# Float32r passes in place of float32 matmuls for the last four score loads of the first batch

## The chip, the cores and the metric

The kernel runs on one core of a Trainium2 chip. The metric is the device time of one execution in microseconds (us); a profile of one execution shows what each engine did in it.

## What is computed

The reference takes `q`, `k` and `v` of 4 batches with 6080 tokens and 256 channels. It attends over channels, not tokens, and sends the result through a feed-forward layer of width 2048:

```python
qn = q / (np.linalg.norm(q, axis=1, keepdims=True) + 1e-06)
kn = k / (np.linalg.norm(k, axis=1, keepdims=True) + 1e-06)
s = kn.transpose(0, 2, 1) @ qn / tau          # 256 x 256 for each batch
a = softmax of s over its last axis
x = (v @ a).reshape(24320, 256)
h = x @ w_in                                  # 256 x 2048
out = (0.5 * h * (1 + erf(h / sqrt(2)))) @ w_out
```

## The kernel before

Work is done batch by batch. For a batch the scores `k^T q` are summed over the tokens, the softmax gives a 256 x 256 matrix, and that matrix is multiplied into `w_in` (`w_group`), so that the tokens of `v` need two products only: the first with the combined weights, then gelu, then the second with `w_out`. The tokens go in six pairs of up to 512-column tiles, and the 2048 hidden channels in 8 units. Products are made of float32r passes: each operand is held as `hi` (the value rounded to float32r, by a copy) and `lo` (the rest, by a subtraction), and three passes lo x hi, hi x hi, hi x lo stand for one float32 product. A float32r pass is one matmul record in the profile; a whole float32 matmul is two.

The scores of batches 1 to 3 are made in this way beside the products of the batch before (`split_qk`, `burst`, lines 178 to 201). Those of the first batch have nothing to run beside. They are made at the start, in a loop of 24 steps (`js`, lines 607 to 620), one for each load of 512 KB (256 tokens of q and k) into a buffer `raw0`, of which there are 13. Step `js` calls `qk_first` (lines 142 to 153): four whole float32 matmuls of 256 columns (line 149) into two PSUM tiles, and for `js` below 20 (`NSQ`) also `squares` (lines 131 to 139): ScalarE squares the load (line 138) and VectorE adds the squares up (line 139). The norms of the tokens of the last four loads come from elsewhere: four pieces of a transposed copy (`norm_part`, line 208 the load, line 209 ScalarE's square with its sum), in a buffer `kq0` of which there are three. Step `js` then issues load `js + 13` (the last four of these are the first loads of batch 1), and at certain steps a norm piece (2, 4, 6, 8), v (5) or a unit of weights (10, 13, 15). Weights come as 64-bit numbers; `narrow` (lines 221 to 251) turns a unit into `hi` and `lo` by a chain of VectorE and ScalarE operations. Steps 14 to 17 also split the first tile pair of v (`v_split`, ScalarE's cast at line 445, VectorE's subtraction at line 446).

After the loop come three more weight units, and `softmax` in stages (line 278): the squares are summed on TensorE (`sum_up`, line 172, held behind the last score matmul), and a chain of small steps on VectorE, ScalarE and TensorE leads to the matrix `eh`, `el`. Between the stages TensorE does part of the scores of batch 1 (`qk_fill`, line 161). Then `w_group` (lines 376 to 379) and the first products (lines 458 to 460), gelu (lines 466 to 468) and the second products (lines 541 to 543) follow, and go on until the end.

All loads and stores are issued from SyncE's queue, in order. The order of an engine's instructions is fixed when the program is built: a scheduler takes, of those whose operands are ready by its own reckoning, the one that comes first in the program.

Of the kernel before, what the change touches and what calls it, by code (L numbers as in the profile page):

```python
# [10 lines left out]
F32R = mybir.dt.float32r  # L11
U32 = mybir.dt.uint32
AF = mybir.ActivationFunctionType
ALU = mybir.AluOpType
AX = mybir.AxisListType

P = 128
B, N, C = 4, 6080, 256
DFF = 2048
NT = 512  # L20
NJ = -(-N // P)
NFT = DFF // P
NCT = C // P
# [7 lines left out]
JS = 2  # L31
# [11 lines left out]
NSQ = 5 * NSJ  # L43
# [9 lines left out]
B11, B21, B22, T1, T2, T3, T4 = range(7)  # L53

A21, B12 = -1, T1
# [5 lines left out]
def channel_attention_gelu_ffn(ctx, tc, qk, kqt, vt, tau, w_in, w_out, out):  # L61
# [11 lines left out]
    nc = tc.nc  # L73
# [5 lines left out]
    pqk = ctx.enter_context(tc.tile_pool(name="pqk", bufs=2))  # L79
# [10 lines left out]
    pst = pstart.__enter__()  # L90

    def f32(ap):
        return ap.bitcast(F32)
# [6 lines left out]
    state = {}  # L100

    marks = {}
# [8 lines left out]
    def bank():  # L111
        return ps_h.tile([P, NT], F32, name="ph")


    raws = {}

    def load_first(i):

        b, js = divmod(i, NQS)
        raw = pst.tile([P, JS, 2, C], F32, name="raw0", bufs=AHEAD)  # L120
        step = 1 if i == 0 else JS
        for j in range(0, JS, step):
            marks["loads"] = nc.sync.dma_start(out=raw[:, j:j + step], in_=qk[b, :, js * JS + j:js * JS + j + step])
        raws[b, js] = raw
# [6 lines left out]
    def squares(js, raw):  # L131
        if js == 0:
            state["acc"] = pst.tile([P, JS, 2, C], F32, name="acc")
            nc.scalar.activation(out=state["acc"], in_=raw, func=AF.Square)
            return
        acc = state["acc"]
        sq = pst.tile([P, JS, 2, C], F32, name="sq", bufs=2)
        nc.scalar.activation(out=sq, in_=raw, func=AF.Square)
        nc.vector.tensor_tensor(out=acc, in0=acc, in1=sq, op=ALU.add)  # L139


    def qk_first(js):
        if js == 0:
            state["s"] = [bank()[:, 0:C] for m in range(NCT)]
        s = state["s"]
        raw = raws.pop((0, js))
        for j in range(JS):
            for m in range(NCT):
                marks["scores"] = nc.tensor.matmul(  # L149
                    s[m], raw[:, j, 0, m * P:(m + 1) * P], raw[:, j, 1],  # L150
                    start=(js == 0 and j == 0), stop=(js * JS + j == NJ - 1), skip_group_check=True)
        if js < NSQ:
            squares(js, raw)

    def qk_fill():
        state["fill"] = s = ps_o.tile([P, NCT, C], F32, name="po")
# [46 lines left out]
    def norm_part(b, t, c):  # L203

        if "nsum" not in state:
            state["nsum"] = pm.tile([P, 2 * NCT, 8], F32, name="nsum")
        x = pst.tile([P, NS], F32, name="kq0", bufs=3) if b == 0 else pg.tile([P, NS], F32, name="kqc", bufs=2)
        nc.sync.dma_start(out=x, in_=kqt[b, t, :, c * NS:(c + 1) * NS])
        nc.scalar.activation(out=x, in_=x, func=AF.Square, accum_out=state["nsum"][:, t, c:c + 1])  # L209
# [199 lines left out]
    def load_v(b, p):  # L409
        t0, n = PAIRS[p]  # L410
        raw = pv.tile([P, NCT, 2 * NT], F32, name="v_raw")
        nc.sync.dma_start(out=raw[:, :, :2 * n],
                          in_=vt[:, b * N + t0:b * N + t0 + 2 * n].rearrange("(t p) n -> p t n", p=P))
        vraw[b, p] = raw

    def v_blocks(b, p):
        n = PAIRS[p][1]
        raw = vraw[b, p]
        return {(k, j): raw[:, k, j * n:(j + 1) * n] for k in range(2) for j in range(2)}
# [15 lines left out]
    def v_split(b, p, i):  # L435
        n = PAIRS[p][1]
        x = v_blocks(b, p)
        src = {B11: x[0, 0], B21: x[1, 0], B22: x[1, 1]}.get(i)
        if (b, p, i) == (0, 0, B12):
            src = x[0, 1]  # L440
        if src is None:
            src = vts[b, p][i - T1][:, :n]
        hi = pv.tile([P, NT], F32R, name=f"vh{i}")
        lo = pv.tile([P, NT], F32R, name=f"vl{i}")
        nc.scalar.copy(out=hi[:, :n], in_=src)
        nc.vector.tensor_tensor(out=lo[:, :n], in0=src, in1=f32(hi[:, :n]), op=ALU.subtract)
        vops[b, p, i] = hi, lo
# [113 lines left out]
    def load_unit():  # L561
        kind, g, d = units.pop(0)
        src = w_in64[:, d, g * NT:(g + 1) * NT] if kind == "in" else w_out64[:, g * 2 * C:(g + 1) * 2 * C]
        loaded.append((kind, g, d, load_w(src)))
# [11 lines left out]
    def narrow_unit():  # L576
        kind, g, d, raw = loaded.popleft()
        if kind == "in":
            if d == 0:
                new_win(0, g)  # L580
            win = wins[0, g]
            narrow(win[:, 0, d], win[:, 1, d], raw)
            if d == NCT - 1:
                keep(keep_in[g], win)
        else:
            new_wo((0, 0, g))
            wo = wos[0, 0, g]
            narrow(wo[:, 0].rearrange("p f c -> p (f c)"), wo[:, 1].rearrange("p f c -> p (f c)"), raw)
            keep(keep_out[g], wo)
# [17 lines left out]
    for js in range(NQS):  # L607
        qk_first(js)
        if js + AHEAD < NQS + FILL:
            load_first(js + AHEAD)  # L610
            if js in (2, 4, 6, 8):
                norm_part(0, *pieces.pop(0))
            if js == 5:
                load_v(0, 0)
        if js in (10, 13, 15):
            load_unit()
        if js in NARROWS:
            narrow_unit()
        if 14 <= js < 18:
            v_split(0, 0, (B11, B21, B12, B22)[js - 14])  # L620
    for _ in range(3):
        narrow_unit()
    for x in held:
# [136 lines left out]
```

## Time and profile before

| | us |
|---|---|
| median of 3 runs | 2186.55 |
| lowest and highest run | 2185.65, 2186.91 |
| the profiled execution | 2186.79 |
| its span, first to last instruction | 2185.0 |
| TensorE busy in it | 2174.5 |
| VectorE busy | 1392.8 |
| ScalarE busy | 1437.0 |

PE is TensorE's matmuls, PEld its weight loads, DVE VectorE, ACT ScalarE, SPq SyncE's queue of transfers. Matmul records overlap their neighbours, so the pace of a series is read from the starts. Times in rows are us from the start of the span, unless marked otherwise.

### The profile page before, as it was taken

Reading aid. Unit: us, or ns where it says so; the run is one execution under the profiler, and the core shown is the slowest. Engines: PE = TensorE matmul, PEld = TensorE weight load, DVE = VectorE, ACT = ScalarE, POOL = GpSimd, SP = SyncE. Lnnn points to the kernel's source line nnn. Section 1 sums busy time; section 2 is a strip of 40 time slices with the busy share of each in tenths; the row PEclk is TensorE's granted clock in tenths of the full one; section 3 lists DMA queues with packets and bytes.
Section 4 is the critical chain, followed back from the end, with each engine's and each line's share of the span. In section 5 each row is a group of like instructions: output and inputs, shape, how many; then the busy total and the mean of one; then the engine's idle time right before and its main releaser. Section 6 shows DMA issues by size and latency. Waiting matters only on the chain.

```text
span 2185.0 us, 26209 instructions
## 1 busy us (share of the span) xinstructions
PE 2174.5 (100%) x9664; PEld 1793.9 (82%) x9664; DVE 1392.8 (64%) x2179; ACT 1437.0 (66%) x2595; POOL 1.3 (0%) x8
## 2 busy tenths in 40 slices
PE   9999999999999999999999999999999999999999
PEld 7788888888888888888888888888888888888888
DVE  6995767656676575675667757657466555555554
ACT  6666666667666666676765666667576566666665
POOL 0000000000000000000000000000000000000000
PEclk9999999999999999999999999999999999999999
DMA  9562534422343353542323335343132122121121
GB/s 380 189 211 106 174 133 157 160 90 87 106 144 105 118 173 116 174 154 67 105 92 134 122 116 174 133 153 128 49 112 97 58 89 71 65 97 66 68 78 47
DMA packets 77056, 267.52 MB, mean 122 GB/s; under 512 B 7680, under 2 KB 9728, under 8 KB 74880
## 3 DMA queue, kind: packets, MB, share of 16 engines
q1 hardware_dynamic: 76928, 265.84, 35.2%
q8 instruction: 76, 1.25, 0.2%
q14 instruction: 52, 0.43, 0.1%
HBM read 232.52 MB, written 33.29 MB: 122 GB/s over the span
## 4 chain that ended last, share of the span: by engine, by line
PE 97%; DVE 2%; DMA 1%; issue 0%; ACT 0%; SPq 0%; DVEq 0%; ACTq 0%
PE po L543 16%; PE po L541 16%; PE po L542 16%; PE ph L460 14%; PE ph L459 14%; PE ph L458 14%; PE ph L191 3%; PE ph L193 1%; DMA raw<-qk 1%; DVE acc L139 1%; PE ph L378 1%; PE ph L376 1%; PE ph L377 1%; PE ph L149 0%; DVE nt L247 0%
## 5 line engine op out<-in xcount | busy, mean ns | idle before, releaser
L468 DVE TENSOR_TENSOR gl<-g,gh 128x512 fp32r<-128x512 f32 (+1 forms) x768 | 521.7, 682 | 145.3 <-ACT g L467 142.7
L543 PE MATMUL po<-gl,wo 128*128 128x512 f32 (+1 forms) x1536 | 605.2, 394 | 0.0
L541 PE MATMUL po<-gh,wo 128*128 128x512 f32 (+1 forms) x1536 | 599.2, 390 | 0.6 <-ACT gh L466 0.6
L542 PE MATMUL po<-gh,wo 128*128 128x512 f32 (+1 forms) x1536 | 595.6, 388 | 0.0
L496 DVE TENSOR_TENSOR h<-ph,p 128x512 f32<-128x512 f32 (+1 forms) x368 | 252.0, 685 | 531.4 <-PE ph L460 452.6
L460 PE MATMUL ph<-vl,wh 128*128 128x512 f32 (+1 forms) x1336 | 522.7, 391 | 0.0
L459 PE MATMUL ph<-vh,wh 128*128 128x512 f32 (+1 forms) x1336 | 521.5, 390 | 0.0
L458 PE MATMUL ph<-vh,wl 128*128 128x512 f32 (+1 forms) x1336 | 519.8, 389 | 0.7 <-DVE wl L363 0.7
L466 ACT ACTIVATE gh<-h 128x512 fp32r<-128x512 f32 (+1 forms) x552 | 345.2, 625 | 236.8 <-DVE h L496 232.8
L491 ACT COPY p<-ph 128x512 f32<-128x512 f32 (+1 forms) x368 | 213.4, 583 | 241.4 <-PE ph L460 240.3
L542 PEld LDWEIGHTS po<-gh,wo 128*128 128x128 f32 x1536 | 288.4, 188 | 64.0
L541 PEld LDWEIGHTS po<-gh,wo 128*128 128x128 f32 x1536 | 288.4, 188 | 62.3 <-ACT gh L466 1.0
L543 PEld LDWEIGHTS po<-gl,wo 128*128 128x128 f32 x1536 | 288.4, 188 | 61.5
L467 ACT ACTIVATE g<-h 128x512 f32<-128x512 f32 (+1 forms) x552 | 337.5, 611 | 0.0
L459 PEld LDWEIGHTS ph<-vh,wh 128*128 128x128 f32 x1336 | 251.1, 188 | 56.9
L458 PEld LDWEIGHTS ph<-vh,wl 128*128 128x128 f32 x1336 | 251.0, 188 | 53.2 <-DVE h L496 1.4
L460 PEld LDWEIGHTS ph<-vl,wh 128*128 128x128 f32 x1336 | 250.9, 188 | 51.0
L491 ACT COPY u<-ph 128x512 f32<-128x512 f32 (+1 forms) x184 | 106.9, 581 | 106.6 <-PE ph L460 106.6
L466 ACT ACTIVATE gh<-ph 128x512 fp32r<-128x512 f32 (+1 forms) x216 | 125.3, 580 | 22.9 <-PE ph L460 18.2
L467 ACT ACTIVATE g<-ph 128x512 f32<-128x512 f32 (+1 forms) x216 | 126.5, 586 | 1.6 <-DVE gl L468 1.5
L496 DVE TENSOR_TENSOR h<-ph,u 128x512 f32<-128x512 f32 (+1 forms) x184 | 125.4, 682 | 2.8
L209 ACT ACTIVATE kqc<-kqc 128x1024 f32<-128x1024 f32 x72 | 76.4, 1061 | 36.1 <-DMA kqc<-kqt 36.0
(135 smaller groups left out, 1354.0 us busy)
## 6 DMA issues: line engine op xcount, KB each, us to landing
wo<-keep_out SPq DMA_DIRECT2D x184, 512.0 KB, 3.3
raw<-qk SPq DMA_DIRECT2D x95, 512.0 KB, 4.3
kqc<-kqt SPq DMA_DIRECT2D x72, 512.0 KB, 4.4
v_raw<-vt SPq DMA_DIRECT2D x20, 1024.0 KB, 5.5
out<-osb SPq DMA_DIRECT2D x40, 512.0 KB, 3.3
win<-keep_in SPq DMA_DIRECT2D x12, 1024.0 KB, 4.8
keep_in<-win SPq DMA_DIRECT2D x4, 1024.0 KB, 4.6
keep_out<-wo SPq DMA_DIRECT2D x8, 512.0 KB, 3.6
```

What stands on the lines that cost most here:

```text
L209: nc.scalar.activation(out=x, in_=x, func=AF.Square, accum_out=state["nsum"][:, t, c:c + 1])
L458: nc.tensor.matmul(ps[:, :n], wl, hi[:, :n], start=start, stop=False, skip_group_check=True)
L459: nc.tensor.matmul(ps[:, :n], wh, hi[:, :n], start=False, stop=False, skip_group_check=True)
L460: marks["product"] = nc.tensor.matmul(ps[:, :n], wh, lo[:, :n], start=False, stop=stop, skip_group_check=True)
L466: nc.scalar.activation(out=gh[:, :n], in_=src, func=AF.Gelu)
L467: marks["gelu"] = nc.scalar.activation(out=g[:, :n], in_=src, func=AF.Gelu)
L468: nc.vector.tensor_tensor(out=gl[:, :n], in0=g[:, :n], in1=f32(gh[:, :n]), op=ALU.subtract)
L491: nc.scalar.copy(out=t[:, :n], in_=ps[:, :n])
L496: nc.vector.tensor_tensor(out=h[:, :n], in0=ps[:, :n], in1=t[:, :n], op=ALU.add)
L541: nc.tensor.matmul(o, wo[:, 1, i, cs], gh[:, :n], start=first, stop=False)
L542: nc.tensor.matmul(o, wo[:, 0, i, cs], gh[:, :n], start=False, stop=False)
L543: nc.tensor.matmul(o, wo[:, 0, i, cs], gl[:, :n], start=False, stop=last)
```

## The change

The last four loads of the first batch (`js` 20 to 23) are split into `hi` (ScalarE's copy) and `lo` (VectorE's subtraction, in a buffer of `kq0`), and `qk_first` multiplies them in three float32r passes. The splits are called in steps 12 to 15, and the splits of v move from steps 14 to 17 to the same steps.

```diff
@@ qk_first
+        if js >= NSQ:
+            hi, lo = halves.pop(js)
+            for j in range(JS):
+                for m in range(NCT):
+                    cs = slice(m * P, (m + 1) * P)
+                    for k, q in ((lo, hi), (hi, hi), (hi, lo)):
+                        marks["scores"] = nc.tensor.matmul(
+                            s[m], k[:, j, 0, cs], q[:, j, 1], start=False,
+                            stop=(js * JS + j == NJ - 1 and q is lo), skip_group_check=True)
+            return
         raw = raws.pop((0, js))
         for j in range(JS):
             for m in range(NCT):
-                marks["scores"] = nc.tensor.matmul(
+                nc.tensor.matmul(
                     s[m], raw[:, j, 0, m * P:(m + 1) * P], raw[:, j, 1],
-                    start=(js == 0 and j == 0), stop=(js * JS + j == NJ - 1), skip_group_check=True)
-        if js < NSQ:
-            squares(js, raw)
+                    start=(js == 0 and j == 0), stop=False, skip_group_check=True)
+        squares(js, raw)
+
+    halves = {}
+
+    def split_first(js):
+        raw = raws.pop((0, js))
+        if js % 2 == 0:
+            state["halves"] = pqk.tile([P, 2, JS, 2, C], F32R, name="hl")
+        hi = state["halves"][:, js % 2]
+        lo = pst.tile([P, JS, 2, C], F32R, name="kq0", bufs=3)
+        nc.scalar.copy(out=hi, in_=raw)
+        nc.vector.tensor_tensor(out=lo, in0=raw, in1=f32(hi), op=ALU.subtract)
+        halves[js] = hi, lo
@@ the loop over js
-        if 14 <= js < 18:
-            v_split(0, 0, (B11, B21, B12, B22)[js - 14])
+        if 12 <= js < 16:
+            v_split(0, 0, (B11, B21, B12, B22)[js - 12])
+            split_first(js + 8)
```

## Rows read from the trace of the kernel before

**Rows 1.** The page, part 1: busy time of each engine (share of the span).

```profile
PE 2174.5 (100%) x9664; PEld 1793.9 (82%) x9664; DVE 1392.8 (64%) x2179; ACT 1437.0 (66%) x2595; POOL 1.3 (0%) x8
```

**Rows 2.** Stretches (us; each engine's busy time (instructions), PEclk, DMA share, GB/s).

```profile
52.20:70.70 18.50, 16.99 (x74) 12.95 (x73) 18.14 (x47) 10.06 (x22) 0.00 (x0) 1.00 0.59 240
...
71.00:2181.00 2110.00, 2109.69 (x9381) 1741.10 (x9382) 1339.29 (x2088) 1394.50 (x2533) 0.00 (x0) 1.00 0.34 115
```

**Rows 3.** The chain that ended last, 38 to 75 us: start, us, what.

```profile
35.94 10.80 DMA raw<-qk
...
46.77 3.72 PE ph L149 x16
50.50 1.69 PE po L172 x16
...
52.21 0.17 DVE small L299
```

**Rows 4.** Stretches, line 149 alone: TensorE and weight loads busy, PEclk, DMA, GB/s.

```profile
3.50:7.50 4.00, 3.78 (x8) 2.52 (x8) 1.00 0.87 265
...
10.60:38.00 27.40, 27.40 (x128) 24.10 (x128) 1.00 1.03 410
...
42.90:50.30 7.40, 7.25 (x32) 5.92 (x32) 1.00 1.03 409
```

**Rows 5.** TensorE in order of time: start, us, what, [idle before it <- releaser].

```profile
7.91 34.47 PE L149 MATMUL ph<-raw 128*128 128x256 f32 x152 [0.47 <-DMA raw<-qk]
42.95 7.55 PE L149 MATMUL ph<-raw 128*128 128x256 f32 x32 [0.57 <-DMA raw<-qk]
50.33 1.84 PE L172 MATMUL po<-ones,acc 128*128 128x1 f32 x16
```

**Rows 6.** SyncE's queue in order of time: loads 22 and 23, then a weight unit.

```profile
35.94 0.96 SPq L123 DMA_DIRECT2D raw<-qk  x2
39.08 0.33 SPq L218 DMA_DIRECT2D raw<-w_in  x1
```

**Rows 7.** TensorE in order of time, a burst of the next batch's scores.

```profile
449.62 0.39 PE L191 MATMUL ph<-hl 128*128 128x512 f32 x1
449.85 0.28 PE L193 MATMUL ph<-hl 128*128 128x256 f32 x1
...
451.70 0.39 PE L191 MATMUL ph<-hl 128*128 128x512 f32 x1
```

**Rows 8.** Instructions by line and shape, 0 to 130 us: count | busy, mean ns.

```profile
L404 DVE TENSOR_TENSOR wl<-hl,wh 128x1024 fp32r<-128x1024 f32 x3 | 3.7, 1220 | 0.2 <-ACT wh L403 0.2
L403 ACT CAST wh<-hl 128x1024 fp32r<-128x1024 f32 x3 | 3.3, 1088 | 0.4 <-DVE hl L399 0.4
```

**Rows 9.** ScalarE in order of time.

```profile
28.94 1.06 ACT L138 ACTIVATE sq<-raw 128x1024 f32<-128x1024 f32 x1 [0.68 <-DVE acc L139]
...
34.36 1.04 ACT L209 ACTIVATE kq<-kq 128x1024 f32<-128x1024 f32 x1
...
39.28 2.16 ACT L445 CAST vh<-v_raw 128x512 fp32r<-128x512 f32 x4
...
42.30 1.04 ACT L209 ACTIVATE kq<-kq 128x1024 f32<-128x1024 f32 x1
...
45.49 1.06 ACT L209 ACTIVATE kq<-kq 128x1024 f32<-128x1024 f32 x1 [2.05 <-DMA kq<-kqt]
```

**Rows 10.** VectorE in order of time.

```profile
42.96 1.22 DVE L139 TENSOR_TENSOR acc<-acc,sq 128x1024 f32<-128x1024 f32 x1
...
49.31 0.43 DVE L234 TENSOR_SCALAR raw<-raw 128x512 f32<-128x512 f32 x1 [2.48 <-DMA raw<-w_in]
```

**Rows 11.** All engines in order of time, 64 to 72 us.

```profile
64.94 0.50 PE L458 MATMUL ph<-vh,wl 128*128 128x512 f32 x1 [0.67 <-DVE wl L363]
...
70.66 0.60 ACT L466 ACTIVATE gh<-ph 128x512 fp32r<-128x512 f32 x1 [2.92 <-DVE wo L251]
...
71.31 0.50 PE L541 MATMUL po<-gh,wo 128*128 128x512 f32 x1 [0.56 <-ACT gh L466]
```

## Prediction

> **What bounds the kernel now.** I read the page first: TensorE is busy for 2174.5 of the 2185.0 us span [rows 1]. From 71 us on there is nothing to find: TensorE is busy for 2109.69 of 2110 us [rows 2], and the change touches no instruction there. It can only move the moment at which that saturated stretch begins. So the whole question is the first 71 us, and there the chain of waits tells what ends last: the transfer of `raw` lands at 46.74, TensorE works through 16 records, sums the squares until 52.19, and VectorE starts the softmax [rows 3]. 16 records are the last two loads, since one whole float32 matmul leaves two records and a load has four matmuls, so 8 records.
>
> Now compare two stretches of TensorE. From 10.6 to 38 us it was full with 128 records, 0.214 us each or 1.71 us a load, while transfers ran at 410 GB/s [rows 4]. There TensorE lagged behind the loads. At 42.95 it waits for load 20, and by the chain for load 22 [rows 3, 5]: it has caught up. At 409 GB/s a 512 KB load takes 1.28 us, less than the 1.71 us of its matmuls, but norm pieces, weights and v lie in the same queue. So the last four loads arrive at a pace that the transfer queue sets, and what counts is the time from the last landing to the end of the scores. It can be dated: load 22 lands at 46.74 [rows 3], load 23 was issued right behind it and a weight load behind that [rows 6], and VectorE sees that weight load at 49.31 [rows 10]. Halfway, load 23 lands at about 48.02. Before, it wasn't even the last: load 22 at 46.74 plus two loads of matmuls ends where the sums begin, 50.33 [rows 5].
>
> **The change part by part.**
>
> Removed: 16 whole float32 matmuls, 32 records, 4 x 1.71 = 6.8 us of TensorE. Added: 4 x 12 passes of 256 columns in float32r. Their pace stands in the batches after the first: pairs of one 512-column and one 256-column pass follow each other at (451.70 - 449.62) / 6 = 0.347 us, the 512-column part taking 0.23, so a 256-column pass takes 0.117 [rows 7]. A load costs 12 x 0.117 = 1.40 us, and 4 x 0.31 = 1.2 us of TensorE work goes. Three short passes in a row, each with a new weight load, stand nowhere in this trace; the bounds are 0.115 below (16 one-column matmuls, weights and all, in 1.84 us [rows 5]) and 0.214 above, the float32 record's. I take 0.117, because half of the rows' passes are exactly this shape.
>
> Most of the removed work was no bound: loads 20 and 21 were waited for. What the change adds is a chain of two operations between landing and first pass. Each load now needs ScalarE's copy to float32r (1.09 us for 128x1024 [rows 8]) and VectorE's subtraction (1.22 us for 128x1024 [rows 8]), and the first pass of each load reads `lo`, the result of both. For load 22: 46.74 + 1.09 + 1.22 + two hand-overs of 0.04 (46.74 to 46.77 [rows 3]) = 49.1, passes until 50.5. For load 23: copy from 48.02 to 49.11, subtraction (VectorE just finished load 22's) to 50.4, TensorE free at 50.5, passes until 51.9. The sums then begin at 51.9 instead of 50.33: **1.6 us later**.
>
> Are the two engines free? ScalarE has only two norm pieces left, at 42.30 and 45.49, and waits 2.05 us for the second [rows 9], so the copies fit between and behind, load 20's perhaps 0.4 us late. VectorE ends its adds at 44.2 and has almost nothing until 49.31 [rows 10]; three subtractions cost nothing there. The fourth ends at 50.4, where the clamp of the next weight unit (49.31) would have run; that moves by at most 1.2 us, into the 2.0 us that VectorE then sat idle until 52.21 [rows 3, 10]. Without that gap, the 1.2 us would be added to a VectorE that is busy 18.14 of the 18.50 us up to the first gelu [rows 2].
>
> Moved: the four splits of v go from steps 14 to 17 to 12 to 15. They began at 39.28 with no idle time before them [rows 9]. ScalarE's other work covers them, and from 46.7 on it has none, so I cost the move at zero; the worst is the 2.2 us of the casts themselves, laid on the squares, and those end 8 us before the sums need them. Buffers: `lo` shares three buffers with the four norm pieces; load 22's waits for the piece at 45.49 + 1.06 = 46.6, before its data is there. Load 23's takes load 20's, free by 47.1. `hi` takes both buffers that the first weight product uses at 62 us, long free. No DMA is added or taken away, SP's queue keeps its order, and the engines behind it run full at 409 to 410 GB/s [rows 4], so the landings stay.
>
> From the sums to the first product (64.94 [rows 11]) the softmax is a chain of small steps, so 1.6 us passes through it. Behind it TensorE has a stall of 0.56 us at 71.31, waiting for the first gelu, and that gelu waited for VectorE's weight work, not for the products [rows 11]. If VectorE's work comes no later, products that end 1.6 us later fill that stall: +1.0. If it comes later by as much, nothing is got back: +1.6. I take **+1.3 us**.
>
> Against the profiled execution (2186.79 us, its span 2185.0 us) that makes 2188.1; against the median of the runs, 2186.55, it makes **2187.9 us**. What a measurement of this kernel tells from no change is about 0.2%, 4.4 us, so this counts as the same.
>
> **The rivals.**
>
> (a) *Absorbed.* VectorE's idle 2.0 us before 52.21 is filled with weight work that now comes in front of the softmax, because ScalarE's square of that unit no longer stands behind the copy of the scores. Then fewer such pieces lie between softmax steps, and the gelu comes earlier. At best all 2.0 us come back: 1.6 - 2.0 = -0.4, 2186.2; with half of it, +0.6. For it: VectorE is busy for 18.14 of 18.50 us there [rows 2], so what leaves that stretch is gained. Against: the order is static, and the program gives the softmax steps high priority (line 627). 20%.
>
> (b) *A slow TensorE after the wait.* Idle from 42.38 [rows 5] to load 20's first pass, 42.95 + 0.4 + 1.09 + 1.22 = 45.7, it waits 3.3 us in place of 0.57. The first 8 records of the kernel, after 3.66 us of nothing, took 3.78 us, 0.47 each against 0.214, about the ratio of 1.2 to 2.4 GHz, though the granted clock of both stretches is shown as 1.00 [rows 4]. The Trainium skill (TensorE: Matmul & The Clock Gate, section "HAM oscillation — how this bites in real kernels") says that waiting for data between bursts of matmuls can put the array back to half rate, so that the next burst starts cold. That rule speaks against this change; the trace agrees only in those first records. If it happens, a pass takes 0.234: loads 20 and 21 run from 45.7 to 51.3, loads 22 and 23 behind them until 54.1 if the clock is then back and 57 if not: 3.8 to 6.5 us late, taken as 2190.5. Against: the wait of 0.67 us before 64.94 left the granted clock at 1.00 [rows 2, 11], though it is far shorter. 10%.
>
> (c) *Copies in front of squares, the slower side.* If ScalarE's order puts load 20's copy where the program writes it, behind the square of step 12 (28.94 [rows 9]), ScalarE stands still until 42.95 and then has 4 copies and 7 squares at 1.05 us each: the last add ends at 42.95 + 11 x 1.05 + 1.22 = 55.7, when the sums began at 50.33; +5.4, and up to +11 with norm pieces and v casts behind. It decides from two squares behind a copy on. Taken as 2192. Against: the first norm piece, written at step 2, ran at 34.36, behind squares of twelve later steps [rows 9], so the order follows arrival. 8%.
>
> (d) *No cheaper passes.* If a short pass costs what the float32 record costs, 0.214 us, a load takes 2.57 us and two from 49.1 end at 54.2: +3.9, 2190.5. Against: [rows 7]. 5%.
>
> **How the numbers follow.** Forecast (+0.6 to +2.0) 57%, (a) 20%, (b) 10%, (c) 8%, (d) 5%. The range runs from 2185.6, (a) at its best less the 0.6 us by which the runs shown differ, to 2190.8, which takes in (d) and the cheaper half of (b); (c) and the rest of (b) stay out. Faster by over 0.2% would need a start 4.4 us shorter, which no case gives: 2%. Slower by over 0.2%: (c) and some of (b), 10%. The same: 88%.
>
> **What would show it.** Right: 48 float32r records at the line of the scores, about 0.117 us apart; load 22 landing at 46.7 still; TensorE idle some 3 us before load 20; VectorE's last subtraction ending near 50.4 and the chain of waits passing through it; the sums beginning near 51.9; the first product near 66.5 with a smaller stall before the first product with `w_out`. Wrong: squares behind 43 us on ScalarE (c), records near 0.23 us (b, d), a weight load landing elsewhere than 49.3, or the sums beginning late while the saturated stretch begins where it did (a).

## The result, and the profile after

The changed kernel takes **2190.44 us**, the median of 21 runs (2189.14 to 2192.48); the kernel before took 2186.32 us in 21 runs beside them (2185.55 to 2187.80). The ratio is 1.0020, 95% interval 1.0014 to 1.0026: 4.1 us or 0.19% slower. That lies inside the range of the prediction and 2.5 us above its value, and the mechanism that the prediction took as the likeliest did not set it. The profiled execution of the changed kernel took 2190.44 us too, its span 2188.6 us against 2185.0. Below line 153 the code moved: whole float32 matmuls of the first batch are now line 159, the passes line 152, the sums of the squares line 195 (172 before), the first product line 481 (458 before).

TensorE in order of time (start, us, what, idle before it and what released it). This answers to [rows 5]:

```profile
10.35 31.35 PE L159 MATMUL ph<-raw 128*128 128x256 f32 x144 [0.67 <-DMA raw<-qk]
45.50 0.58 PE L152 MATMUL ph<-hl,kq 128*128 128x256 f32 x1 [3.80 <-DVE kq L174]
45.88 0.42 PE L152 MATMUL ph<-hl 128*128 128x256 f32 x1
...
50.79 0.41 PE L152 MATMUL ph<-hl,kq 128*128 128x256 f32 x1
51.01 0.35 PE L152 MATMUL ph<-hl 128*128 128x256 f32 x1
51.19 0.28 PE L152 MATMUL ph<-kq,hl 128*128 128x256 f32 x1
...
53.78 1.84 PE L195 MATMUL po<-ones,acc 128*128 128x1 f32 x16
...
64.70 0.50 PE L399 MATMUL ph<-win,eh 128*128 128x512 f32 x1 [1.00 <-ACT eh L366]
...
68.70 0.50 PE L481 MATMUL ph<-vh,wl 128*128 128x512 f32 x1 [0.96 <-DVE wl L386]
```

TensorE runs out of whole matmuls at 41.70 (10.35 + 31.35) and waits 3.80 us for load 20's subtraction. Then come 48 passes at two paces. From 45.88 to 50.79 there are 23 steps, 4.91 / 23 = 0.2135 us each; from 51.19 on they are 0.118 apart. The sums begin at 53.78, 3.45 us later than before [rows 5].

The same stretch in windows (from:to us, length, busy time of TensorE, weight loads, VectorE, ScalarE, GpSimd with instructions, granted clock, DMA share, GB/s):

```profile
43.00:46.00 3.00, 0.50 (x2) 0.50 (x3) 2.77 (x3) 3.00 (x5) 0.00 (x0) 0.72 1.02 404
46.00:48.00 2.00, 2.00 (x11) 2.00 (x11) 1.49 (x3) 2.00 (x4) 0.00 (x0) 0.50 1.03 414
48.00:50.00 2.00, 2.00 (x12) 2.00 (x11) 1.86 (x3) 0.10 (x1) 0.00 (x0) 0.50 1.02 401
50.00:52.00 2.00, 2.00 (x14) 2.00 (x14) 1.21 (x3) 0.69 (x1) 0.00 (x0) 0.72 1.04 416
52.00:54.00 2.00, 2.00 (x20) 2.00 (x18) 0.00 (x0) 0.37 (x2) 0.00 (x0) 1.00 1.04 420
...
71.00:2184.00 2113.00, 2112.56 (x9394) 1743.13 (x9393) 1342.08 (x2093) 1392.75 (x2532) 0.00 (x0) 1.00 0.34 115
```

The granted clock stands at 0.50, the 1.2 GHz level, just where the passes are 0.2135 us apart, and at 1.00 where they are 0.118. TensorE counts as busy for 2.00 of 2.00 us throughout: busy time alone does not show a slow clock, the number of instructions in a window does (11 and 12 against 20). From 71 us on TensorE is full, as before [rows 2].

The clock was low in more than the profiled execution. Its mean over an execution is 0.999 in 13 of the changed kernel's 21 runs (median 2190.01 us) and 0.998 in the other 8 (median 2191.64), and 1.000 in all 80 runs of the kernel before that were taken beside the experiments.

What the passes waited for stands in ScalarE's and VectorE's rows, in order of time. First ScalarE:

```profile
41.16 1.05 ACT L138 ACTIVATE sq<-raw 128x1024 f32<-128x1024 f32 x1
42.12 1.04 ACT L232 ACTIVATE kq<-kq 128x1024 f32<-128x1024 f32 x1
...
43.16 1.97 ACT L173 CAST hl<-raw 128x1024 fp32r<-128x1024 f32 x2
45.04 1.05 ACT L232 ACTIVATE kq<-kq 128x1024 f32<-128x1024 f32 x1
...
46.09 2.00 ACT L173 CAST hl<-raw 128x1024 fp32r<-128x1024 f32 x2
```

Then VectorE:

```profile
44.22 2.36 DVE L174 TENSOR_TENSOR kq<-raw,hl 128x1024 fp32r<-128x1024 f32 x2 [0.23 <-ACT hl L173]
...
47.16 2.59 DVE L174 TENSOR_TENSOR kq<-raw,hl 128x1024 fp32r<-128x1024 f32 x2 [0.51 <-ACT hl L173]
49.67 0.42 DVE L257 TENSOR_SCALAR raw<-raw 128x512 f32<-128x512 f32 x1
...
55.66 0.16 DVE L322 TENSOR_TENSOR small<-po,small 128x4 f32<-128x4 f32 x1 [4.12 <-PE po L195]
```

ScalarE has no gap from the last square (41.16) to the last copy, so load 20's copy could not start before 43.16. Its copy and subtraction end at 45.46, and TensorE starts at 45.50.

**One sum fits nearly all runs.** Span = start of the sums + TensorE's marked idle behind them + the rest, which is saturated work. All numbers are from the profiled execution of each kernel. The burst is the run of score matmuls of the last four loads, in e11 of the last two; the clock is the lowest mean of a window of about 2 us:

| kernel | wait before the burst | clock, 42 to 52 us | sums begin | idle behind | span | rest |
|---|---|---|---|---|---|---|
| before | 0.57 | 1.00 | 50.33 | 0.84 + 0.67 + 0.56 | 2185.0 | 2132.6 |
| after | 3.80 | 0.50 | 53.78 | 1.00 + 0.96 | 2188.6 | 2132.9 |
| e1 | 0.40 | 1.00 | 51.31 | 1.05 + 0.97 | 2186.1 | 2132.8 |
| e8 | 2.67 | 0.54 | 54.37 | 0.53 | 2186.8 | 2131.9 |
| e9 | 0.54 | 1.00 | 49.25 | 0.84 + 0.67 + 0.55 | 2184.6 | 2133.3 |
| e2 | none | 1.00 | 49.30 | 0.96 + 0.29 + 0.52 + 1.16 | 2185.0 | 2132.8 |
| e6 | 3.93 | 0.50 | 54.45 | 1.95 | 2189.3 | 2132.9 |
| e4 | 1.68 | 1.00 | 49.67 | 0.62 + 1.64 + 1.02 + 1.19 | 2187.4 | 2133.3 |
| e11 | 2.25 | 0.50 | 52.24 | 1.94 | 2187.6 | 2133.4 |
| e12 | 3.50 | 0.50 | 54.72 | 1.83 | 2189.4 | 2132.9 |
| e14 | none | 1.00 | 50.33 | 0.42 + 4.04 + 0.32 | 2189.0 | 2133.9 |
| e15 | 4.32 | 0.56 | 54.81 | 3.56 + 0.24 + 0.81 | 2194.9 | 2135.5 |

So the 3.6 us by which the span grew are 3.45 of later sums, -0.11 of idle and 0.3 that the sum leaves open. The experiments divide the 3.45. In this table only e14 and e15 leave more than 1 us open; both have a slow clock behind the sums as well. Two profiles of kernels without the chain, e9 and e2, begin their sums 1.0 to 1.1 us sooner than the kernel before, though neither is measurably faster: a difference of 1 us in that column is no finding by itself.

### The profile page after: what moved, and what is told of

Read it like the earlier page. It is cut to its first block, busy times and chain, and to the rows that moved or that the text cites. A ratio compares the mean times of both kernels' runs of the same rounds, so it can differ in the third digit from the quotient of the medians.

```text
span 2188.6 us, 26253 instructions
## 1 busy us (share of the span) xinstructions
PE 2174.1 (99%) x9680; PEld 1795.6 (82%) x9680; DVE 1397.6 (64%) x2183; ACT 1439.4 (66%) x2599; POOL 1.3 (0%) x8
## 3 DMA queue, kind: packets, MB, share of 16 engines
q8 instruction: 76, 1.25, 0.2%
## 4 chain that ended last, share of the span: by engine, by line
PE 96%; DVE 2%; DMA 1%; ACT 1%; issue 0%; SPq 0%; DVEq 0%
PE po L566 16%; PE po L564 16%; PE po L565 16%; PE ph L483 14%; PE ph L482 14%; PE ph L481 14%; PE ph L214 3%; PE ph L216 1%; DMA v_raw<-vt 1%; DVE acc L139 1%; PE ph L399 1%; PE ph L401 1%; PE ph L400 1%; PE ph L152 0%; DMA raw<-qk 0%
```

## The experiments

Two theories stood against each other. **Clock**: the wait for load 20's split lowers TensorE's clock, and the passes start at half pace. **Chain** (the forecast): copy and subtraction behind the last landing set the end. Side theories were short passes that are never cheaper, VectorE's subtractions, and the move of v's splits. The ratios below are against runs of the kernel before on the same chip (medians of 2186.3 to 2186.5 us).

### e1: TensorE kept busy in the wait

Eight float32 matmuls of load 19's data into a tile that nobody reads are added ahead of the passes.

```diff
         if js >= NSQ:
             hi, lo = halves.pop(js)
+            if js == NSQ:
+                warm = ps_o.tile([P, NT], F32, name="po")
+                for i in range(8):
+                    nc.tensor.matmul(warm[:, 0:C], state["last"][:, i % 2, 0, 0:P], state["last"][:, i % 2, 1],
+                                     start=True, stop=True, skip_group_check=True)
...
         squares(js, raw)
+        state["last"] = raw
```

> The changed kernel with eight whole float32 matmuls of load 19 into a PSUM tile that nothing reads, placed in the wait before load 20's passes (16 records, 3.4 us of the 3.8 us wait). Theory W (the wait drops TensorE's clock, and the half rate until 51 us costs about 2.5 us): granted clock 1.00 throughout, the 48 passes 0.117 us apart, the sums beginning at 51.1 to 51.4 in place of 53.78, and the kernel 1.5 to 2.5 us faster than the changed one, 2188.0 to 2189.0. Rival C (the chain of copy and subtraction alone makes it late): sums at 53.8, 2190.4 again.

Measured: 2188.34 us (2187.90 to 2189.19, 11 runs), ratio 1.0011, interval 1.0002 to 1.0020. TensorE in order of time:

```profile
41.31 3.62 PE L151 MATMUL po<-raw 128*128 128x256 f32 x16
45.33 0.38 PE L157 MATMUL ph<-hl,kq 128*128 128x256 f32 x1 [0.40 <-DVE kq L180]
45.55 0.28 PE L157 MATMUL ph<-hl 128*128 128x256 f32 x1
...
51.19 0.28 PE L157 MATMUL ph<-kq,hl 128*128 128x256 f32 x1
51.31 1.84 PE L201 MATMUL po<-ones,acc 128*128 128x1 f32 x16
```

and two of its windows:

```profile
46.00:48.00 2.00, 2.00 (x19) 2.00 (x18) 1.38 (x3) 1.90 (x3) 0.00 (x0) 1.00 1.02 410
48.00:50.00 2.00, 2.00 (x17) 1.83 (x16) 1.97 (x4) 0.17 (x1) 0.00 (x0) 1.00 1.02 401
```

The passes start almost where they did (45.33), at 1.00 and 0.117 us apart, and the sums begin 2.47 us sooner than after the change, though TensorE does more. The medians differ by 2.1 us, and the mean clock is 1.000 in all 11 runs. What remains against the kernel before is 51.31 - 50.33 = 0.98 us of later sums in the two profiled executions, but 2.0 us between the medians (2188.34 against 2186.32): e1's profiled execution, 2187.90, is the fastest of its 11. It is put down to the chain, the part of the change that is left; against e2 below, which makes the same splits but does not wait for them, e1's sums come 2.01 us later.

### e8: whole float32 matmuls behind the same chain

Each of the last four loads is multiplied by whole float32 matmuls of `lo` and `hi`, so that they wait for the same subtraction. For these loads the kernel computes lo x hi alone.

```diff
-                    for k, q in ((lo, hi), (hi, hi), (hi, lo)):
-                        marks["scores"] = nc.tensor.matmul(
-                            s[m], k[:, j, 0, cs], q[:, j, 1], start=False,
-                            stop=(js * JS + j == NJ - 1 and q is lo), skip_group_check=True)
+                    marks["scores"] = nc.tensor.matmul(
+                        s[m], f32(lo)[:, j, 0, cs], f32(hi)[:, j, 1], start=False,
+                        stop=(js * JS + j == NJ - 1), skip_group_check=True)
```

> The changed kernel with each load's three passes replaced by one whole float32 matmul of lo and hi (so it computes lo x hi alone for the last four loads), which waits for the same copy and subtraction. It tells the wait from the short passes. Theory W (the wait alone drops the clock): granted clock 0.50 from about 46 to 51, the first 12 or so records 0.43 us apart and the rest 0.214, 32 records from 45.5 to about 55, 2191 to 2193. Rival P (the short float32r passes with their dense weight loads are what is slow or what the throttle answers): clock 1.00, records 0.214 apart, sums at 52.4, 2188 to 2189.

Measured: 2188.51 us (2187.13 to 2190.47, 11 runs), ratio 1.0011, interval 1.0002 to 1.0019. TensorE in order of time, and its windows:

```profile
45.67 8.86 PE L151 MATMUL ph<-hl,kq 128*128 128x256 f32 x32 [2.67 <-DVE kq L173]
54.37 1.84 PE L194 MATMUL po<-ones,acc 128*128 128x1 f32 x16
```

```profile
46.00:48.00 2.00, 2.00 (x7) 1.58 (x6) 1.50 (x3) 2.00 (x4) 0.00 (x0) 0.54 1.04 416
48.00:50.00 2.00, 2.00 (x7) 1.66 (x6) 1.44 (x2) 0.24 (x1) 0.00 (x0) 0.61 1.01 397
50.00:52.00 2.00, 2.00 (x11) 1.74 (x11) 1.67 (x4) 0.69 (x1) 0.00 (x0) 1.00 1.04 414
```

The clock falls for float32 records too, seven of them in 2 us in place of eleven. So it is the wait that lowers it, not the short passes with their many weight loads; the mean clock is below 1.000 in 10 of the 11 runs. The sums begin later than after the change (54.37), yet the total is about as in e1, below the 2191 to 2193 that were expected: only 0.53 us of idle follows. VectorE, held up longer, ran three more steps of a weight unit ahead of the softmax, and its later stalls went. That is the prediction's rival *Absorbed*, seen in a kernel of a different order; after the change itself it was worth only 0.11 us.

### e2 and e9: the split without its use

e2 makes the splits and multiplies the raw data by whole float32 matmuls; e9 leaves out the subtractions as well (the last line of the diff is e9's alone).

```diff
-            hi, lo = halves.pop(js)
+            hi, lo, raw = halves.pop(js)
...
-                    for k, q in ((lo, hi), (hi, hi), (hi, lo)):
-                        marks["scores"] = nc.tensor.matmul(
-                            s[m], k[:, j, 0, cs], q[:, j, 1], start=False,
-                            stop=(js * JS + j == NJ - 1 and q is lo), skip_group_check=True)
+                    marks["scores"] = nc.tensor.matmul(
+                        s[m], raw[:, j, 0, cs], raw[:, j, 1], start=False,
+                        stop=(js * JS + j == NJ - 1), skip_group_check=True)
...
         nc.scalar.copy(out=hi, in_=raw)
-        nc.vector.tensor_tensor(out=lo, in0=raw, in1=f32(hi), op=ALU.subtract)
```

> The changed kernel with the splits still made but not read: the last four loads are multiplied as whole float32 matmuls from the raw load. Theory W: copies and subtractions lie in gaps of ScalarE and VectorE and cost nothing themselves; sums at 50.0 to 50.5 as in the kernel before, 2186.0 to 2187.0. Rival V (the added work on VectorE and ScalarE is what delays the softmax): sums at 50.3, but the first product 1 us or more later than the 64.94 of before, and 2187.5 or more.

> The run with unused splits without the subtractions: the last four loads are multiplied whole, ScalarE still makes the four copies, VectorE nothing more than before. It asks where the 1.5 us of that run came from, whose sums began 1 us earlier than in the kernel before. If VectorE's 4.8 us of subtractions cost it, by moving the weight work behind the first softmax steps: the first clamp of the weight unit comes before the softmax again and the time is 2186.0 to 2186.8. If it is the spread between executions, or the copies: 2187.3 to 2188 again.

Measured: e2 2187.78 us (2186.46 to 2189.01, 11 runs), ratio 1.0007, interval 0.9998 to 1.0016; e9 2186.38 us (2185.45 to 2187.19, 11 runs), ratio 1.0001, interval 0.9992 to 1.0010. VectorE in order of time, e9:

```profile
48.18 0.43 DVE L255 TENSOR_SCALAR raw<-raw 128x512 f32<-128x512 f32 x1 [2.32 <-DMA raw<-w_in]
...
51.13 0.16 DVE L320 TENSOR_TENSOR small<-po,small 128x4 f32<-128x4 f32 x1 [2.05 <-PE po L193]
```

and e2:

```profile
47.84 2.36 DVE L173 TENSOR_TENSOR kq<-raw,hl 128x1024 fp32r<-128x1024 f32 x2 [0.51 <-ACT hl L172]
51.18 0.16 DVE L321 TENSOR_TENSOR small<-po,small 128x4 f32<-128x4 f32 x1 [0.99 <-PE po L194]
51.26 0.42 DVE L256 TENSOR_SCALAR raw<-raw 128x512 f32<-128x512 f32 x1
```

The copies cost nothing: the median of e9 equals that of the kernel before. With the subtractions, the sums begin just as early (49.30 and 49.25), but the clamp of the next weight unit comes behind the first softmax step (51.26) instead of ahead of it (48.18), and TensorE's idle behind the sums grows from 2.06 to 2.93 us. The medians differ by 1.4 us; the intervals overlap, and e2's profiled execution (2186.76) is 1.0 us faster than its median, so the cost is likely, not certain. In the changed kernel the clamp ran at 49.67, ahead of that step, so this cost did not arise there.

### e6 and e4: the splits of v

e6 puts the splits of v back to steps 14 to 17 (the upper part of the diff). e4 leaves them in steps 12 to 15 and issues the load of v behind load 23 (the lower part), so that the last loads can land earlier and ScalarE is free for their copies.

```diff
         if 12 <= js < 16:
-            v_split(0, 0, (B11, B21, B12, B22)[js - 12])
             split_first(js + 8)
+        if 14 <= js < 18:
+            v_split(0, 0, (B11, B21, B12, B22)[js - 14])
...
-            if js == 5:
+            if js == 10:
```

> The changed kernel with the splits of v back in steps 14 to 17. Theory W: they run when v has landed wherever they are written, so load 20's copy starts at 43.2 and its passes at 45.5 as in the changed kernel, and the time is the same, 2190 to 2191. Rival M (the move puts the v splits in front of load 20's copy): the copy starts up to 2.1 us earlier, the wait falls below 2 us, and 2188 or less.

> The changed kernel with v's first load issued behind load 23, not in step 5: loads 20 to 23 land 2.56 us earlier, and the casts of v no longer stand in front of load 20's copy on ScalarE. Theory W: the wait in front of load 20 falls from 3.8 us to 1.5 to 2 us, the clock stays at 1.00, the sums begin at 48.5 to 50, before those of the kernel before (50.33), and the time falls by 2.5 us or more against the changed kernel, to 2186 to 2188, with up to 2.5 us given back where the splits of v now fall into VectorE's busy stretch. Rival C: the passes still take until 53 or the time stays at 2190.

Measured: e6 2190.67 us (2189.34 to 2191.30, 11 runs), ratio 1.0019, interval 1.0011 to 1.0028; e4 2189.97 us (2189.20 to 2190.84, 11 runs), ratio 1.0018, interval 1.0009 to 1.0027. So e6 is as slow as the change: ScalarE runs the casts of v at the same place, and the move costs nothing. TensorE of e4 in order of time:

```profile
43.69 0.39 PE L152 MATMUL ph<-hl,kq 128*128 128x256 f32 x1 [1.68 <-DVE kq L174]
...
49.67 1.84 PE L195 MATMUL po<-ones,acc 128*128 128x1 f32 x16
...
59.76 0.41 PE L362 MATMUL po<-ident,e 128*128 128x128 f32 x2 [1.64 <-ACT e L353]
```

and VectorE of e4:

```profile
52.16 0.68 DVE L469 TENSOR_TENSOR vl<-v_raw,vh 128x512 fp32r<-128x512 f32 x1
```

A wait of 1.68 us left the clock at 1.00 (its mean is 1.000 in 10 of the 11 runs), and the sums begin 0.66 us *earlier* than in the kernel before. That the shorter passes did this is not shown: e2 and e9 begin theirs at 49.30 and 49.25 with whole matmuls. The total is no better, and above the 2186 to 2188 that were expected, because the subtractions of v, three of them from 52.16 on, now run in VectorE's fullest stretch. Idle behind the sums rises to 4.47 us. What is gained ahead of the sums is lost again where VectorE is made to pay for it.

### e11 and e12: two loads alone

e11 splits loads 22 and 23 only, e12 loads 20 and 21 only (with (20, 21) in the diff's place of (22, 23)); the other two are multiplied whole, by lines that the diff leaves out.

```diff
...
-            split_first(js + 8)
+            if js + 8 in (22, 23):
+                split_first(js + 8)
```

> Half of the change: loads 20 and 21 stay whole float32 matmuls, loads 22 and 23 are split and multiplied in passes. TensorE then works on load 20 as soon as it lands, and the wait moves in front of load 22 and gets shorter, some 2.5 us. Theory W (the length of the wait decides through the clock): if that wait is short enough the clock stays at 1.00, the sums begin at 51.0 to 52.0 and the kernel is at 2187.5 to 2188.5, as with the wait filled; a wait of 2.67 us did lower it in the run before this one, and then the sums begin at 53 to 54 and it is 2190 or more. Rival C (chain alone): sums at 51.9 with the clock at 1.00 whatever the wait.

> The other half: loads 20 and 21 are split and multiplied in passes, loads 22 and 23 stay whole, so the last landing has no chain behind it. Theory W: the wait in front of load 20 is as long as in the changed kernel (3.8 us), the clock is 0.50 from about 46 to 51, 24 passes at 0.2135 last until 50.6, the whole matmuls follow until about 54; sums at 53.5 to 54.5 and 2190 to 2191.5, as slow as the whole change. Rival C: 24 passes at 0.117 from 45.5 end at 48.3, the whole matmuls at 51.7; sums at 51.7, 2188.

Measured: e11 2189.08 us (2187.56 to 2190.47, 11 runs), ratio 1.0012, interval 1.0003 to 1.0021; e12 2191.24 us (2190.22 to 2192.57, 10 runs), ratio 1.0022, interval 1.0013 to 1.0032. TensorE of e11 in order of time, and its windows:

```profile
47.78 0.43 PE L160 MATMUL ph<-hl,kq 128*128 128x256 f32 x1 [2.25 <-DVE kq L182]
...
52.24 1.84 PE L203 MATMUL po<-ones,acc 128*128 128x1 f32 x16
```

```profile
46.00:48.00 2.00, 0.22 (x1) 0.22 (x2) 1.45 (x2) 1.52 (x2) 0.00 (x0) 1.00 1.04 418
48.00:50.00 2.00, 2.00 (x11) 2.00 (x11) 1.77 (x3) 0.62 (x1) 0.00 (x0) 0.50 1.01 401
```

TensorE of e12:

```profile
45.55 0.58 PE L160 MATMUL ph<-hl,kq 128*128 128x256 f32 x1 [3.50 <-DVE kq L182]
...
50.84 4.05 PE L151 MATMUL ph<-raw 128*128 128x256 f32 x16
54.72 1.51 PE L203 MATMUL po<-ones,acc 128*128 128x1 f32 x13
```

In this execution 2.25 us of waiting were enough to lower the clock (0.50 from 48 to 50 us), though the sums begin sooner than the 53 to 54 expected for that case. It was not so in each: the mean clock is 0.999 in three of e11's 11 runs (the profiled one is among them; median 2190.43 us) and 1.000 in the other eight (median 2188.81). So this kernel's median is 1.6 us higher where the clock fell. In e12 the 24 passes of two loads take from 45.55 to 50.84, 5.29 us at the low clock: 0.22 us a pass, when the 16 records they replace took 0.214 each, 3.4 us. Splitting the first two loads is by itself as slow as splitting all four.

### e14 and e15: last loads earlier

Three of the four norm pieces are issued behind load 23, which lets loads 20 to 23 come earlier. e14 does this to the kernel *before*, without any split. e15 does it to the changed kernel and also moves the four subtractions to GpSimd (the lower part of the diff).

```diff
-            if js in (2, 4, 6, 8):
+            for _ in range({2: 1, 10: 3}.get(js, 0)):
...
-        lo = pst.tile([P, JS, 2, C], F32R, name="kq0", bufs=3)
+        lo = pst.tile([P, JS, 2, C], F32R, name="raw0", bufs=AHEAD)
         nc.scalar.copy(out=hi, in_=raw)
-        nc.vector.tensor_tensor(out=lo, in0=raw, in1=f32(hi), op=ALU.subtract)
+        nc.gpsimd.tensor_tensor(out=lo, in0=raw, in1=f32(hi), op=ALU.subtract)
```

> The kernel before, with three of the four norm pieces issued behind the loads of step 10 instead of in steps 4, 6 and 8, so that loads 20 to 23 have up to three transfers of 512 KB (3 x 1.28 us) fewer in front of them. Nothing of the change is in it. Theory: TensorE then does not wait for load 20 (before: 0.57 us at 42.95) and works on at 1.71 us a load, so the sums can begin up to 0.57 us earlier, about 49.8, unless the later norm pieces or the last square hold them; total 2185.5 to 2186.5 beside 2186.4, no difference that can be measured. If the last four loads were not bound by their transfers at all, the wait stays. If the order of VectorE's weight work against the softmax decides, the total goes up by 1 to 2 us although the sums begin no later.

> The changed kernel with the same three norm pieces issued behind step 10, and the four subtractions on GpSimd (lo in the buffers of the loads), so that VectorE is spared and the last loads land up to 3.8 us earlier. Theory (the wait before load 20's passes drops the clock): the copy of load 20 still stands behind ScalarE's squares, v casts and pieces and cannot begin long before 41 to 42; GpSimd's subtraction of 128x1024 has no row in any trace here, and is at least VectorE's 1.22 us. If it is 1.2 to 2 us, TensorE waits 2 to 4 us, the clock drops again, and the sums begin at 52 to 54: 2188 to 2190. If it is 2.5 us or more, the four subtractions in a row (10 us) set the end: sums at 54 or later, 2190 to 2193. Rival (VectorE's subtractions are what costs): with VectorE spared the total falls to 2186 to 2187 whatever the clock does.

Measured: e14 2190.11 us (2189.14 to 2191.28, 11 runs), ratio 1.0017, interval 1.0008 to 1.0025; e15 2196.48 us (2195.93 to 2197.06, 5 runs), ratio 1.0044, interval 1.0030 to 1.0058. TensorE of e14 in order of time, and a window:

```profile
8.52 41.98 PE L149 MATMUL ph<-raw 128*128 128x256 f32 x184 [1.25 <-DMA raw<-qk]
50.33 1.84 PE L172 MATMUL po<-ones,acc 128*128 128x1 f32 x16
...
62.63 0.41 PE L339 MATMUL po<-ident,e 128*128 128x128 f32 x2 [4.04 <-ACT e L330]
```

```profile
64.00:66.00 2.00, 2.00 (x6) 1.53 (x6) 2.00 (x5) 1.98 (x3) 0.00 (x0) 0.50 0.00 0
```

VectorE of e14:

```profile
53.02 0.16 DVE L298 TENSOR_REDUCE small<-nsum 128x4 f32<-128x4 f32 x1 [8.55 <-ACT kq L209]
```

The wait for load 20 is gone, as expected: 184 records without a gap. This execution began its matmuls 0.61 us later (8.52 against 7.91 [rows 5]) and ran them at half pace, 0.43 us a record, until 12.1 us, which hides the gain. Then the edit hurts elsewhere, by far more than the 1 to 2 us expected at worst: the small step that needs the last norm piece stands in VectorE's queue ahead of the weight unit, and VectorE does nothing for 8.55 us. The work held up there makes TensorE wait 4.04 us in the softmax, and behind *that* wait the clock is at 0.50 as well; its mean is below 1.000 in all 11 runs. This kernel holds nothing of the change, so the same thing happens with other instructions in another place.

GpSimd of e15 in order of time, then its VectorE:

```profile
42.75 10.49 POOL L174 TENSOR_TENSOR raw<-raw,hl 128x1024 fp32r<-128x1024 f32 x4 [40.88 <-ACT hl L173]
```

```profile
49.11 1.89 DVE L257 TENSOR_SCALAR raw<-raw 128x512 f32<-128x512 f32 x1
51.04 2.49 DVE L262 TENSOR_SCALAR nt<-raw 128x512 uint32<-128x512 uint32 x1
```

Four subtractions take GpSimd 10.49 us, 2.6 each against VectorE's 1.22 [rows 8]. TensorE waits 4.32 us, the clock falls to 0.56, and the sums begin at 54.81. The total is above every range in the expectation. Sparing VectorE did not help, so the rival as it was written falls, though this kernel is too slow elsewhere to say what VectorE's subtractions alone are worth.

No run beat the kernel before; e9, which equals it, splits to no purpose.

## Why the prediction came out as it did

That the time lies in the range is luck as far as the forecast's own mechanism goes: that mechanism gave +0.6 to +2.0 us, +4.1 were measured, and the upper end of the range stood where it did for the sake of rivals (b) and (d).

- **What bounds it: right.** Behind 71 us TensorE is full in both kernels, and the whole difference is in the first 69 us.
- **The landings: nearly right.** The last two loads were issued at 35.75 (35.94 before [rows 6]). ScalarE began load 22's copy at 46.09 without having to wait for it, so it had landed at least 0.65 us before the 46.74 of [rows 3]. In e9, with whole matmuls, it landed at 45.64; why the landings move by that much no run tells.
- **The chain behind the last landing: right in kind, 1.6 us forecast, 1.0 to 2.0 measured (e1).** Between the profiled executions it is 0.98, and the missing 0.6 us is about what load 22 came earlier by; between the medians all that e1 leaves is 2.0. The durations held: a copy took 1.04 and a subtraction 1.22 us on average, against 1.09 and 1.22 [rows 8].
- **"A pass takes 0.117": the step that failed.** The prediction priced all 48 passes at the full clock. That holds in e1 (0.117) and not here, where 26 of the 48 passes took 0.2135, as long as the float32 record at the full clock [rows 4]. 26 x (0.2135 - 0.117) = 2.5 us, which is the difference between the sums after the change and in e1, 53.78 - 51.31 = 2.47. With the chain's 0.6 less between these profiles, 0.2 less idle got back than forecast and the 0.3 that stays open this makes 2.3 us: the profiled execution (2190.44) stands 2.3 us above the 2188.1 that the prediction gave against the profiled one.
- **Rival (b), slow TensorE: this is what happened,** and it was given 10%. Its working was close: first pass at 45.7 (measured 45.50), sums at 54.1 if the clock came back in time (53.78), total 2190.5 (2190.44). In part that is luck: it took 0.234 us for a slow pass and 24 of them, where 0.2135 and 26 were measured. What was misjudged is the evidence. The kernel's first records, at half pace behind a wait of 3.66 us, stood in the trace and spoke for it [rows 4]; what was set against it was a wait of 0.67 us [rows 11], a fifth of the 3.3 us that the same paragraph had worked out. That the view shows 1.00 over those first records was no argument for the full clock: in e14 it shows 1.00 too where records are 0.43 us apart. The Trainium skill (TensorE: Matmul & The Clock Gate, section "HAM oscillation — how this bites in real kernels") says that waiting for data between bursts can make the next one start at half rate; the profiled executions agree, with windows at 0.50 to 0.56 behind waits of 2.25 to 4.32 us.
- **Rivals (c) and (d) fell.** ScalarE's last square began at 41.16, ahead of all copies; and in e1 the short passes are cheaper than the records, 1.40 us a load against 1.71.
- **VectorE's subtractions at nothing: right for this kernel, as far as its rows show.** The clamp came at 49.67 instead of 49.31, inside the gap. e2 shows that the cover is thin: with the order turned round, 0.87 us more idle follows.
- **The moved splits of v at nothing: right** (e6).
- **The gelu's stall: half right.** The 0.56 us at 71.31 is gone, as forecast, and so is one of 0.84 in the softmax, but a new wait of 1.00 us for `eh` (64.70) took its place, and that at the first product grew from 0.67 to 0.96. Of the 0.3 us that were to come back, 0.11 did.

## What to carry to other kernels

Where a change puts a wait of a few microseconds in front of a burst of matmuls, price the burst at both clock levels, and trust the trace's row with the nearest wait, not the shortest. Work taken from TensorE in a stretch that the transfers pace is no gain; the time counts from the last landing, and each operation between landing and matmul adds to it. Filler matmuls in the wait (e1) gave back 2.1 us here; no run found a use of the passes that was better than whole matmuls, which open no such wait.

## What the runs showed of the hardware

- In the profiled executions, waits of 0.40, 0.57, 0.85 (e15, before load 23), 1.00, 1.05, 1.16 (e2), 1.19 (e4), 1.64, 1.68 and 1.83 us (e12, before its first product) left the granted clock at 1.00 where the next burst ran; behind waits of 2.25, 2.67, 3.50, 3.56 (e15, in the softmax), 3.80, 3.93, 4.04 and 4.32 us it was 0.50, or 0.54 to 0.56 in windows in which it changed.
- From one execution of a kernel to the next the outcome varied. The mean clock is below 1.000 in 3 of e11's 11 executions (its wait is 2.25 us in the profiled one), in 10 of 11 of e8 (2.67 us) and in 1 of 11 of e4 (1.68 us). How long the wait was in the executions that were not profiled is not known.
- At the start of an execution the view's clock cannot be relied on: e14 runs at 0.43 us a record from 8.52 to 12.1 us behind a wait of 1.25 us, twice the later 0.214, with 1.00 shown. The first records of the kernel before are the same case [rows 4].
- The clock stayed low under full load: after the change 26 passes, 45.50 to 51.01 us, ran at half pace with TensorE busy throughout.
- In e15 VectorE's clamp and its neighbour took 1.89 and 2.49 us while GpSimd worked on SBUF, against 0.42 and 0.43 after the change (the clamp 0.43 before [rows 10]). GpSimd's last subtraction runs from 50.7 to 53.24, and the two end at 51.00 and 53.53, each just behind a subtraction. So they look blocked, not slowed; that was read from one trace and not tried by itself. The Trainium skill (SBUF — State Buffer, section "SBUF: two separate sides") says that GpSimd's instructions and some of VectorE's take a shared pair of ports for a whole instruction, with the other engine blocked; this trace agrees.
